# A Fourier-filter and gated-MLP block: small scale arithmetic moved to GpSimd, the first tiles transposed in fp32, and a later clock for DMA

## The chip, the cores and the metric

The kernel runs on one core of one Trainium2 chip. Five engines work side by side on it, each through a queue of its own in program order: TensorE (PE, matmuls into PSUM), VectorE (DVE), ScalarE (ACT), GpSimd (POOL) and SyncE (SP), which here issues all DMAs. The metric is device time in microseconds (us) of one execution. Three runs of the kernel before took 435.36, 435.87 and 436.03 us; the median, 435.87, is the time before.

## The reference

The input x has 2048 tokens of 448 values. Three terms are added:

```python
xn = (x - mean) / sqrt(var + 1e-5)                      # per token
y1 = irfft2(rfft2(xn) * (w_r + 1j * w_i))               # over tokens and features
gate, up = x @ W_gate, x @ W_up                         # of xn, 448 -> 1792
y2 = ((gate * (gate > 0)) * up) @ W_down                # 1792 -> 448
out = x + y1 + y2                                       # fp32
```

The gated MLP is fed with xn. All operands and the result are fp32.

## The kernel before

**Precision by halves.** A matrix is held as two fp16 parts, hi (the value rounded to fp16) and lo (the remainder). A product takes three fp16 matmuls, hi x hi, lo x hi and hi x lo. Weights are first scaled by a power of two, found from their sum of squares.

**The MLP.** The 1792 hidden features are 14 slabs f of 128, taken in groups of 5, 5 and 4. Tokens are 16 tiles n2 of 128, in four chunks q of four tiles (n2 = q, q+4, q+8, q+12), in the order 0, 2, 1, 3. A gate-and-up unit (`gu`) multiplies one slab with one chunk: for gate (g = 0) and up (g = 1) ten matmuls of 512 columns, and a group on half the rows (`gu_halves`) that two neighbouring units share. ScalarE and VectorE turn the sums into h (relu, product, hi, lo). When a group's slabs are done for a chunk, four down-projection units (`dn`) follow, one a tile. They add into a PSUM bank that ScalarE first seeds with the running output (`dn_seed`) and then reads back (`dn_post`).

**The filter.** The two-dimensional transform runs as small DFT matmuls (`f_dft`, `f_sdft`, `i_sdft`, `i_ddft`, PSUM tile fx) and butterflies on VectorE (tile y). It is background work, laid between the MLP's units.

**Tokens.** The MLP needs the normalized tokens transposed: `Tq[q]` holds nine blocks of 128 features by 512 tokens. Blocks 0 to 2 are hi, 5 to 7 lo; blocks 3, 4 and 8 hold the 64 last columns, their lo, and a strided choice of columns. For the first chunk (`CHUNKS[0]`, tiles 0, 4, 8, 12) TensorE transposes; for the other three a DMA does. The first chunk's steps before, named as in the list `OPENING`: `lx` load, `bn`, `ag` mean and variance, `sq` root on ScalarE, `ra` to `rm` the reciprocal root on VectorE in small steps (groups A: tiles 0, 4; B: 8, 12; C: chunk 2), `xn` (or `an` on ScalarE) the normalized tile, `hi` its fp16 half (on ScalarE, from the loaded tile), `lo` the remainder on VectorE, `tpA` and `tpB` three fp16 transposes each, `evA` and `evB` the copies out of PSUM, `tpC` and `evC0` to `evC2` the 64 last columns of all four tiles.

**The opening.** `OPENING` (line 34) is written out by hand: each engine runs the pieces of its own in that order. Weights of the first group: `lw` loads the next half slab, `wsqWfg` sums its squares on ScalarE, `parWf` adds them over partitions on GpSimd, `wexW` and `wscW` take the power of two on VectorE, `whiW` (ScalarE) and `wloW` (VectorE) write the halves. The first matmuls of slab 0 are cut into three 256-column ones each: `hh`, `lh`, `hl`, first digit g, second digit the half of the chunk; `ml` and `hp` handle the last columns. `guFgG` is ten matmuls of slab F. `re`, `tm`, `gh`, `gl` are the four steps to h. `lwd`, `wdq`, `wdp`, `wdsc`, `wdh`, `wdl` are the same for the down projection's weights. `warm` and `kw4` are matmuls on zeros.

**Behind the opening** a planner (`Order`, line 183) decides. It has a cost for each instruction, runs all queues against each other on paper (`place`), picks by due time and earliest start, and issues every instruction in the order that comes out. Cost and start time are its own estimates. A DMA counts as landed by `dma`; an instruction that needs it may start 0.04 us later (`lag`, line 317). How much background work is laid beside a unit follows from `V_US` and `room`.

Line 413 is the one line that issues all planned instructions, so the profile shows L413 nearly everywhere; groups are told apart by tile names. wst, wt: weight slabs as loaded and as halves; wdst, wdt: the same for the down projection; wds, dsc, dinv: its scales; wsc: a slab's power of two; xy: tokens and running output; T: `Tq`; arena: a shared area with, among others, the token tiles of the opening, constants and DFT tables; gu, dn, fx: PSUM.

Of the kernel before, what the change touches and what calls it, by code (L numbers as in the profile page):

```python
# [25 lines left out]
NWARM = 16  # L26
ARENA = 17072
HOLD = 3.0
# [6 lines left out]
lx0 lx4 bn0 lx12 bn4 lx8 lw ag0 lid lw ag4 sqA raA rbA rcA warm rdA rmA xn0 bn12 bn8 an4 ag12 hi0 ag8 lo0 hi4 sqB tpA0  # L35
wsqW0g0 lx14 lw tpB0 raB lo4 rbB rcB tpB4 kw4 rdB rmB aevA0 wsqW0g1 lw xn8 tpA4 parW0g0 wexW0g0 lx6 lw vevB4 hi8 vevB0
hi12 wscW0g0 vevA4 whiW0g0 lx10 tpA8 aevA8 tpA12 parW0g1 lo8 tpB8 wsqW1g1 hh00 hl00 wsqW1g0 lw lw lw xn12 vevA12 hh01
lo12 wexW0g1 wloW0g0 parW1 wscW0g1 tpB12 whiW0g1 vevB12 lx2 tpC aevC1 bn6 lwd3 lh01 lh00 wexW1 wscW1 vevB8 hh10 vevC0
whiW1g0 wloW0g1 hl10 wloW1g0 whiW1g1 wloW1g1 hl11 bn10 bn2 bn14 hh11 lwd0 wsqW3g1 ml0 ml1 wsqW2g0 wsqW2g1 lh11 wsqW3g0
parW2 lfd ag2 hl01 ag10 lh10 ag14 ag6 hp0 re0 tm0 lw lwd1 sqC raC wexW2 lw gu1g0 rbC wscW2 rcC rdC xn14 parW3 wexW3  # L40
whiW2g1 wloW2g1 lwd4 gu1g1 hi14 cp14 wscW3 xn2 whiW2g0 lo14 wloW2g0 whiW3g0 hi2 lwd2 whiW3g1 wsqW4g0 xn10 re1 wsqW4g1
parW4 wloW3g0 hi10 cp2 ly0 tm1 gu2g1 gu2g0 cp10 ly4 wdq0 wdq4 wloW3g1 wexW4 gh0 xn6 wdq3 lo10 hp2 gu3g0 hi6 re2 ly12
wscW4 whiW4g0 lo2 whiW4g1 gu3g1 lo6 wdq2 gh1 tm2 dm14 wdq1 gl0 wloW4g0 gu4g0 ly8 dm10 wloW4g1 gl1 cp6 gu4g1 re3 gh2
tm3 wdp wdsc gh3 gl3 aevC2 wdh1 dm2 gl2 wdl1 wdh4 dm6 wdh3 wdl4 hp4 re4 wdl3 tm4 wdh0 wdl0 wdh2 wdl2 gh4 gl4
# [60 lines left out]
def _constants():  # L105
# [55 lines left out]
    ident = np.eye(128, dtype=np.float16)  # L161
# [9 lines left out]
class _Node:  # L171
    __slots__ = ("eng", "ops", "key", "run", "fixed", "after", "wait", "users", "start", "ready", "late")
# [10 lines left out]
class Order:  # L183
# [5 lines left out]
    SWITCH = 0.093  # L189

    def __init__(self, hold):
        self.nodes, self.reads, self.writes, self.masks = [], {}, {}, {}
        self.key, self.after, self.fixed, self.group, self.hold, self.stream = 0.0, None, True, None, hold, []
# [17 lines left out]
    @contextmanager  # L211
    def run(self, back=True):
        n = self.node("P")
        n.run = back
        self.group = n
        yield n
        self.group = None
# [84 lines left out]
    def place(self):  # L302
# [37 lines left out]
        def pick(e):  # L340
# [25 lines left out]
            if h[1] > t + 0.5 or soon and (mode[0] != (128, 128) or now - n.ready > self.hold):  # L366
# [51 lines left out]
def tile_gfnet_reglu(ctx: ExitStack, tc: tile.TileContext, x, xr, wgu, wd, wf, ident, c_fd, c_fm, c_im, c_row, c_id,  # L418
                     out):
    nc = tc.nc  # L420
    order = Order(HOLD)
# [107 lines left out]
    id_t = ft([128, 128], F16, "id_t")  # L529
# [78 lines left out]
    def ln_r(step, q, js=(0, 1, 2, 3)):  # L608
# [3 lines left out]
        if step == "a":  # L612
            V.reciprocal(r0, sd)
        elif step == "b":
            V.scalar_tensor_tensor(t, m[:, :, 1], 1e-5, r0, op0=OP.add, op1=OP.mult)
        elif step == "c":
            V.scalar_tensor_tensor(t, t, -0.5 * 2048, r0, op0=OP.mult, op1=OP.mult)
        elif step == "d":
            V.scalar_tensor_tensor(r, t, 1.5 * 2048, r0, op0=OP.add, op1=OP.mult)
        elif q == CHUNKS[0]:  # L620
            V.scalar_tensor_tensor(nm, m[:, :, 0], -1.0, r, op0=OP.mult, op1=OP.mult)
        elif q in CHUNKS[2:]:
            V.tensor_scalar(nm, m[:, :, 0], -1.0, None, op0=OP.mult)
# [9 lines left out]
    for t in tts:  # L633
        G.memset(t[:, 3:9:5, 64:128], 0.0)
# [5 lines left out]
    def ln_xn(n2, act=False):  # L640
        xn_b[n2] = free.pop(0)
        xn[n2] = flat(xn_b[n2])[:, 0:D]
# [33 lines left out]
    def ln_lo(n2):  # L676
# [41 lines left out]
    def ln_ev(n2, part, act):  # L718
        q, j = n2 % 4, n2 // 4
        copy(Tq[q][:, 5 * part:5 * part + 3, 128 * j:128 * (j + 1)], tp[n2, part][:, 0:3], act)  # L720

    def ln_tpc(q):

        b = (fx(), fx())
        for i in range(3):
            tp["end", i] = b[i // 2].bitcast(F16)[:, 512 * (i % 2):512 * (i % 2) + 512]
        for j in range(4):
            t = tt[q + 4 * j].rearrange("p a b -> p (a b)")
            c, l = t[:, 384:448], t[:, 1024:1088]
            for i, half in enumerate(((c, t[:, 7:512:8]), (l, c), (l, t[:, 647:1152:8]))):  # L730
                for h in range(2):
                    P.transpose(tp["end", i][64 * h:64 * h + 64, 128 * j:128 * j + 128], half[h], id_t)

    def ln_evc(q, i, act):
        copy(Tq[q][:, (3, 4, 8)[i], :], tp["end", i], act)
# [412 lines left out]
    def i_ddft(a, b):  # L1148
# [6 lines left out]
        with order.run():  # L1155
# [78 lines left out]
    def wd_scale(g, fs):  # L1234
# [564 lines left out]
```

## Time and profile before

| | |
|---|---|
| median of three runs | 435.87 us (435.36 to 436.03) |
| the profiled execution | 435.47 us |
| its span, first to last instruction | 433.7 us |
| granted TensorE clock, mean | 0.999 |
| busy: PE, DVE, ACT, POOL | 425.0, 383.9, 262.6, 29.9 us |
| DMA | 38.63 MB, mean 89 GB/s |

A row of a timeline gives start, length, engine, line, operation, output<-input, shape and count of instructions that follow each other, and in brackets the engine's idle time ahead of it with what ended it. A row of groups gives a count, then the busy time in us and the mean of one in ns, then the idle time. A row of waits gives the total in us, the number of times and the longest. PEld is the loading of weights, which overlaps PE. Matmuls overlap as well: one of 512 columns lasts 0.379 us but the next starts 0.216 later.

### The profile page before, as it was taken

What the parts mean: (1) busy time and instruction counts of PE and PEld (TensorE: products, weight loads), DVE (VectorE), ACT (ScalarE), POOL (GpSimd) and SP (SyncE); (2) the same over time, 40 slices, a digit from 0 to 9 for tenths busy, and PEclk for the clock granted to TensorE, in tenths of its full rate; (3) what the DMA queues carried; (4) which work ended last, traced back from release to release, by engine and by line L of the source; (5) the groups of instructions that cost most, each with busy time, mean ns of one, the idle gap of its engine ahead of it and who ended that gap; (6) DMA issues with size and microseconds to landing.
All of it is one profiled execution on the core that took longest, in us unless ns stands there. A gap on an engine that the chain in (4) does not pass through costs nothing.

```text
span 433.7 us, 8470 instructions
## 1 busy us (share of the span) xinstructions
PE 425.0 (98%) x3222; PEld 202.7 (47%) x3222; DVE 383.9 (89%) x804; ACT 262.6 (61%) x495; POOL 29.9 (7%) x72
## 2 busy tenths in 40 slices
PE   7999999999999999999999999999999999999996
PEld 2644544444444444445444444444454554544554
DVE  6998989999998899899999999999999999973443
ACT  5898466387448658545534634764756765864761
POOL 1140013042000200000000000100000000000000
PEclk9999999999999999999999999999999999999999
DMA  8859319009104532342504200030222220210212
GB/s 259 297 123 264 127 46 239 7 14 227 42 3 132 182 101 86 89 127 79 158 14 108 82 1 0 16 86 2 51 47 50 73 74 16 80 44 2 85 44 87
DMA packets 37721, 38.63 MB, mean 89 GB/s; under 512 B 18928, under 2 KB 33072, under 8 KB 37680
## 3 DMA queue, kind: packets, MB, share of 16 engines
q1 hardware_dynamic: 37680, 38.09, 31.4%
q8 instruction: 25, 0.41, 0.4%
q14 instruction: 16, 0.13, 0.1%
HBM read 23.20 MB, written 3.67 MB: 62 GB/s over the span
## 4 chain that ended last, share of the span: by engine, by line
PE 42%; DVE 36%; issue 9%; ACT 4%; DMA 4%; SPq 2%; POOL 2%; DVEq 0%; ACTq 0%; POOLq 0%
PE gu L413 27%; DVE y L413 17%; PE dn L413 11%; DVE arena L413 5%; PE fx L413 4%; DVE g L413 3%; DVE h L413 3%; DVE wst L413 3%; SPq L413 2%; DVE wt L413 2%; POOL arena L413 2%; ACT arena L413 1%; DMA arena<-in_wf 1%; DMA xy<-in_x 1%; ACT junk L413 1%
## 5 line engine op out<-in xcount | busy, mean ns | idle before, releaser
L413 PE MATMUL gu<-T,wt 128*128 128x512 f16 (+2 forms) x1250 | 264.6, 376 | 0.0
L413 PEld LDWEIGHTS <-wt 128*128 128x128 f16 (+1 forms) x1250 | 111.3, 97 | 143.5 <-issue 20.9
L413 PE MATMUL dn<-wdt,h 128*128 128x448 f16 x648 | 125.6, 353 | 1.4 <-ACT dn L413 1.4
L413 PEld LDWEIGHTS <-h 128*128 128x128 f16 x684 | 66.0, 98 | 63.2 <-issue 4.1
L413 ACT ACTIVATE h<-g 128x512 f16<-128x512 f32 x56 | 35.1, 628 | 60.3 <-DVE g L413 59.9
L413 DVE TENSOR_TENSOR y<-y 128x464 f32<-128x464 f32 (+2 forms) x82 | 59.0, 745 | 2.7 <-ACT y L413 1.8
L413 DVE TENSOR_TENSOR arena<-arena 128x116 f32<-128x116 f32 (+6 forms) x105 | 53.2, 525 | 4.2 <-ACT arena L413 2.8
L413 DVE SCALAR_TENSOR_TENSOR g<-gu,g 128x512 f32<-128x512 f32 x56 | 38.3, 684 | 18.8 <-ACT g L413 15.8
L413 ACT ACTIVATE g<-gu 128x512 f32<-128x512 f32 x56 | 32.8, 586 | 32.4 <-PE gu L413 32.4
L413 DVE TENSOR_TENSOR h<-g,h 128x512 f16<-128x512 f32 x56 | 38.4, 687 | 4.4 <-ACT h L413 3.7
L413 ACT ACTIVATE xy<-dn,dsc 128x448 f32<-128x448 f32 x44 | 27.5, 626 | 19.4 <-PE dn L413 19.1
L413 DVE TENSOR_TENSOR wst<-wst 128x116 f32<-128x116 f32 (+2 forms) x96 | 30.8, 374 | 0.6
L413 DVE SCALAR_TENSOR_TENSOR y<-y 128x232 f32<-128x232 f32 (+2 forms) x52 | 30.1, 600 | 0.7
L413 ACT ACTIVATE dn<-xy,dinv 128x448 f32<-128x448 f32 x44 | 27.7, 636 | 1.9 <-DMA xy<-in_x 0.8
L413 PEld LDWEIGHTS <-arena 64*128 64x128 f16 (+2 forms) x836 | 17.1, 96 | 14.4 <-issue 5.5
L413 ACT ACTIVATE wt<-wst,wsc 128x512 f16<-128x512 f32 x28 | 18.9, 710 | 4.0 <-DVE wsc L413 4.0
L413 DVE SCALAR_TENSOR_TENSOR wt<-wst,wsc,wt 128x512 f16<-128x512 f32 x28 | 20.2, 744 | 0.1
L413 POOL COPY arena<-arena 128x56 f16<-128x56 f16 (+1 forms) x36 | 15.8, 474 | 59.7 <-ACT arena L413 53.8
L413 ACT ACTIVATE junk<-wst 128x512 bf16<-128x512 f32 x28 | 17.4, 622 | 3.5 <-DMA wst<-in_wgu 3.1
L413 ACT ACTIVATE arena<-arena 128x116 f32<-128x116 f32 (+3 forms) x33 | 14.9, 463 | 7.5 <-DMA arena<-in_wf 5.2
L413 POOL PARTITION_ALL_REDUCE wm<-wm x15 | 8.2, 547 | 158.4 <-ACT junk L413 158.4
L413 PE MATMUL fx<-arena 64*128 64x64 f16 (+3 forms) x484 | 17.8, 245 | 0.8 <-DVE T L413 0.5
(81 smaller groups left out, 294.6 us busy)
## 6 DMA issues: line engine op xcount, KB each, us to landing
wst<-in_wgu SPq DMA_DIRECT2D x28, 256.0 KB, 4.7
arena<-in_wf SPq DMA_DIRECT2D x16, 232.0 KB, 2.9
arena<-y SPq DMA_DIRECT2D x64, 58.0 KB, 2.0
arena<-wst SPq DMA_DIRECT2D x32, 116.0 KB, 2.2
y<-in_xr SPq DMA_DIRECT2D x16, 224.0 KB, 4.2
xy<-in_x SPq DMA_DIRECT2D x16, 224.0 KB, 3.6
out<-xy SPq DMA_DIRECT2D x15, 224.0 KB, 1.9
wdst<-in_wd SPq DMA_DIRECT2D x14, 224.0 KB, 3.4
```

Of the source, the lines that this page charges most:

```text
L413: fn(*a, **k)
```

## The change

Four things are done.

1. **First token tiles.** `xn` of tiles 0, 4, 8 and 12 stays fp32 in the memory of the fp16 tiles (`xts`). Three fp32 transposes a tile (`ln_tp`, identity now fp32, 64 KB) go to four PSUM banks; ScalarE's copy rounds to hi (`ath`), VectorE subtracts hi from PSUM for lo (`tl`). The 64 last columns take eight fp32 matmuls with the identity (`ln_tpc`), a copy (`aend0`), two subtractions (`end2`, `end3`) and one DMA inside SBUF (`end1`). `hi`, `lo`, `evA`, `evB`, `evC`, `an` of these tiles go. Zeroings are split: part stays at the start, one a tile (`z0` to `z3`) comes behind `tpC`.
2. **Small operations.** `shift_exponent` runs on GpSimd except for slabs 0 and 1. The root steps `rb` to `rm` of the chunks other than the first run there as one or two operations each. In `wd_scale` the products and maxima go there; the exponent, the reduction over features and the reciprocals stay on VectorE.
3. **The planner.** For an instruction behind the opening that is not a DMA itself, a DMA counts as landed 0.8 us after its estimate instead of 0.04 (`SLACK`). The hold time is given by kind of run, with the value of before for each; fp32 matmuls and 64-column ones get costs of their own; `V_US` gets smaller costs for the moved steps.
4. **The list.** `OPENING` is written anew: 10 warm-up matmuls instead of 16, `kw4` gone, other places for loads and weights.

```diff
-NWARM = 16
+NWARM = 10
-HOLD = 3.0
+HOLDS = 3.0, 3.0, 3.0, 3.0
...
 OPENING = """
+lx0 warm lx4 bn0 bn4 ag0 ag4 sqA raA rbA lx8 rcA rdA xn0 lx12 bn8 lw wsqW0g0 lid bn12 lw ag8 tp0 ag12 sqB xn4 wsqW0g1
+parW0g0 raB rbB ath0 lw wexW0g0 tp4 rcB rdB lw wscW0g0 xn8 whiW0g0 xn12 tp8 tl0 wloW0g0 parW0g1 tp12 rmA wsqW1g0 tpC
+ath4 wexW0g1 wsqW1g1 wscW0g1 whiW0g1 hh00 parW1 tl4 lh00 ath12 ath8 aend0 lx2 wexW1 hh10 wloW0g1 hl00 hh01 wscW1 tl8
+whiW1g0 hh11 tl12 lh11 whiW1g1 end2 wloW1g0 z2 wloW1g1 lwd3 lw lw lh01 lw lw wsqW3g1 hl11 lx6 lx14 end1 lx10 bn6 lwd0
+lwd2 wsqW2g0 lw lh10 wsqW2g1 hl10 parW2 bn10 bn2 hl01 wsqW3g0 z0 wexW2 ml1 bn14 ml0 hp0 ag2 parW3 wscW2 gu1g1 ag10 re0
+whiW2g1 lwd1 wexW3 ag14 ag6 sqC lw tm0 lfd wloW2g1 whiW2g0 raC wscW3 whiW3g0 rbC lwd4 rmB z3 rcC wsqW4g0 gu1g0 whiW3g1
+wloW2g0 wsqW4g1 rdC gu2g0 wloW3g0 xn14 hi14 z1 cp14 re1 wdq0 xn2 wloW3g1 lo14 ly4 parW4 xn10 tm1 hi2 cp2 hi10 wexW4
...
-    ident = np.eye(128, dtype=np.float16)
+    ident = np.eye(128, dtype=np.float32)
...
+    SLACK = 0.8
...
-            return max([d.end + 0.04 for d in op.deps if not (pe and d.node.eng == "P")], default=0.0)
+            far = 0.04 if op.node.eng == "S" or op.node.fixed else self.SLACK
+            return max([d.end + (far if d.node.eng == "S" else 0.04) for d in op.deps
+                        if not (pe and d.node.eng == "P")], default=0.0)
...
-    def shift_exponent(o, e, sign, n):
+    def shift_exponent(o, e, sign, n, E=G):
-        V.tensor_scalar(o.bitcast(U32), e.bitcast(U32), float(sign), n * EXPONE, op0=OP.mult, op1=OP.add)
+        E.tensor_scalar(o.bitcast(U32), e.bitcast(U32), float(sign), n * EXPONE, op0=OP.mult, op1=OP.add)
...
         elif step == "b":
-            V.scalar_tensor_tensor(t, m[:, :, 1], 1e-5, r0, op0=OP.add, op1=OP.mult)
+            G.tensor_scalar(t, m[:, :, 1], 1e-5, None, op0=OP.add)
+            G.tensor_tensor(t, t, r0, op=OP.mult)
         elif step == "c":
-            V.scalar_tensor_tensor(t, t, -0.5 * 2048, r0, op0=OP.mult, op1=OP.mult)
+            G.tensor_tensor(t, t, r0, op=OP.mult)
+            G.tensor_scalar(t, t, -0.5 * 2048, 1.5 * 2048, op0=OP.mult, op1=OP.add)
         elif step == "d":
-            V.scalar_tensor_tensor(r, t, 1.5 * 2048, r0, op0=OP.add, op1=OP.mult)
+            G.tensor_tensor(r, t, r0, op=OP.mult)
...
+    def ln_tp(n2):
+        j = n2 // 4
+        b = (side[1], *side[0], side[2])[j]
+        tp[n2] = b[:, 0:384].rearrange("p (a b) -> p a b", b=128)
         for a in range(3):
-            P.transpose(tp[n2, part][:, a, :], tt[n2][:, 5 * part + a, :], id_t)
+            P.transpose(tp[n2][:, a, :], xn[n2][:, 128 * a:128 * a + 128], id_t)
...
+    def ln_th(n2, act):
+        js = slice(128 * (n2 // 4), 128 * (n2 // 4) + 128)
+        copy(Tq[n2 % 4][:, 0:3, js], tp[n2], act)
+    def ln_tl(n2):
+        T, js = Tq[n2 % 4], slice(128 * (n2 // 4), 128 * (n2 // 4) + 128)
+        V.tensor_tensor(T[:, 5:8, js], tp[n2], T[:, 0:3, js], op=OP.subtract)
...
+        tp["end"] = side[1]
+        for j, x in enumerate(xts):
+            js = slice(128 * j, 128 * j + 128)
+            for h, c in ((0, slice(384, 448)), (1, slice(7, 512, 8))):
+                P.matmul(tp["end"][64 * h:64 * h + 64, js], x[:, c], id_t, start=j == 0, stop=True,
+                         skip_group_check=True)
+    def ln_end(q, i, act=False):
+        T, a = Tq[q], tp["end"]
+        if i == 0:
+            copy(T[:, 3, :], a, act)
+        elif i == 1:
+            Q.dma_start(T[64:128, 4, :], T[0:64, 3, :])
+        elif i == 2:
+            V.tensor_tensor(T[0:64, 4, :], a[0:64], T[0:64, 3, :], op=OP.subtract)
+        else:
+            V.tensor_tensor(T[:, 8, :], a, T[:, 3, :], op=OP.subtract)
...
-        V.tensor_tensor(sc[:, 0, 0:n], w[:, :, 0], w[:, :, 1], op=OP.mult)
-        V.scalar_tensor_tensor(sc[:, 1, 0:n], sc[:, 0, 0:n], 2.0 ** -64, e, op0=OP.max, op1=OP.mult)
+        G.tensor_tensor(sc[:, 0, 0:n], w[:, :, 0], w[:, :, 1], op=OP.mult)
+        G.tensor_scalar(sc[:, 1, 0:n], sc[:, 0, 0:n], 2.0 ** -64, None, op0=OP.max)
+        G.tensor_tensor(sc[:, 1, 0:n], sc[:, 1, 0:n], e, op=OP.mult)
         V.tensor_reduce(sc[:, 2, 0:1], sc[:, 1, 0:n], axis=AX.X, op=OP.max)
-        V.tensor_scalar(dsc[:, g:g + 1], sc[:, 2, 0:1], 2.0 ** -20, 2.0 ** -60, op0=OP.mult, op1=OP.max)
+        G.tensor_scalar(dsc[:, g:g + 1], sc[:, 2, 0:1], 2.0 ** -20, 2.0 ** -60, op0=OP.mult, op1=OP.max)
...
-    V_US = {"w_scale": 0.2, "w_lo": 0.66, "wd_scale": 1.1, "wd_lo": 0.6}
+    V_US = {"w_scale": 0.1, "w_lo": 0.66, "wd_scale": 0.7, "wd_lo": 0.6}
```

More of the change, by code (lines that the diff above doesn't have):

```diff
@@ L34 @@
 OPENING = """
[L35 to L44, printed above, removed]
+lx0 warm lx4 bn0 bn4 ag0 ag4 sqA raA rbA lx8 rcA rdA xn0 lx12 bn8 lw wsqW0g0 lid bn12 lw ag8 tp0 ag12 sqB xn4 wsqW0g1
[5 more added lines that the diff above has]
+wloW2g0 wsqW4g1 rdC gu2g0 wloW3g0 xn14 hi14 z1 cp14 re1 wdq0 xn2 wloW3g1 lo14 ly4 parW4 xn10 tm1 hi2 cp2 hi10 wexW4
+cp10 gh0 xn6 hi6 gu2g1 lo10 wscW4 ly12 lo2 hp2 re2 lo6 ly8 gh1 tm2 wdq4 gl0 dm14 dm10 wdq3 gl1 gu3g0 whiW4g0 wdq2 cp6
+whiW4g1 wloW4g0 gu3g1 end3 wdq1 wloW4g1 re3 gh2 tm3 wdp wdsc gh3 dm2 gu4g0 gu4g1 dm6 gl3 wdh1 gl2 ly0 wdl1 hp4 wdh4
+wdh3 wdl4 re4 tm4 wdl3 wdh0 wdl0 wdh2 gh4 gl4 wdl2
 """
@@ L171 @@
 class _Node:
-    __slots__ = ("eng", "ops", "key", "run", "fixed", "after", "wait", "users", "start", "ready", "late")
+    __slots__ = ("eng", "ops", "key", "run", "fixed", "after", "wait", "users", "start", "ready", "hold", "late")
 def _repeat(m, step, n):
@@ L189, with __init__ @@
     SWITCH = 0.093
-    def __init__(self, hold):
+    SLACK = 0.8
+    def __init__(self):
         self.nodes, self.reads, self.writes, self.masks = [], {}, {}, {}
-        self.key, self.after, self.fixed, self.group, self.hold, self.stream = 0.0, None, True, None, hold, []
+        self.key, self.after, self.fixed, self.group, self.stream = 0.0, None, True, None, []
     def engine(self, eng, real):
@@ L211, in run @@
     @contextmanager
-    def run(self, back=True):
+    def run(self, hold=None):
         n = self.node("P")
-        n.run = back
+        n.run, n.hold = hold is not None, hold
         self.group = n
@@ L365, in pick @@
             soon = t <= now + self.SWITCH + 0.01
-            if h[1] > t + 0.5 or soon and (mode[0] != (128, 128) or now - n.ready > self.hold):
+            if h[1] > t + 0.5 or soon and (mode[0] != (128, 128) or now - n.ready > n.hold):
                 return run
@@ L632, in tile_gfnet_reglu @@
     tts = [ft([128, 9, 128], F16, f"tt{i}") for i in range(4)]
-    for t in tts:
-        G.memset(t[:, 3:9:5, 64:128], 0.0)
+    xts = [t.rearrange("p a b -> p (a b)").bitcast(F32) for t in tts]
+    for t, u in zip(tts, xts):
+        G.memset(u[:, 448:512], 0.0)
+        G.memset(t[:, 8, 64:128], 0.0)
     def new_tt(n2):
@@ L640, in ln_xn @@
     def ln_xn(n2, act=False):
-        xn_b[n2] = free.pop(0)
-        xn[n2] = flat(xn_b[n2])[:, 0:D]
+        if n2 % 4 == CHUNKS[0]:
+            xn[n2] = xts[n2 // 4][:, 0:D]
+        else:
+            xn_b[n2] = free.pop(0)
+            xn[n2] = flat(xn_b[n2])[:, 0:D]
         r, nm, mean = rst[n2 % 4, n2 // 4, "r"]
@@ L716, in copy @@
             V.tensor_copy(o, i)
-    def ln_ev(n2, part, act):
-        q, j = n2 % 4, n2 // 4
-        copy(Tq[q][:, 5 * part:5 * part + 3, 128 * j:128 * (j + 1)], tp[n2, part][:, 0:3], act)
-    def ln_tpc(q):
[L724 to L735, printed above, removed]
+    def ln_th(n2, act):
[4 more added lines that the diff above has]
+        V.tensor_tensor(T[:, 5:8, js], tp[n2], T[:, 0:3, js], op=OP.subtract)
+    def ln_tpc(q):
+        tp["end"] = side[1]
[12 more added lines that the diff above has]
+            V.tensor_tensor(T[0:64, 4, :], a[0:64], T[0:64, 3, :], op=OP.subtract)
+        else:
+            V.tensor_tensor(T[:, 8, :], a, T[:, 3, :], op=OP.subtract)
     fi, sfx = {}, {}
@@ L776, in f_dft @@
         ps, T = fx2(), Tq[a % 4]
-        with order.run():
+        with order.run(HOLDS[0]):
             for k, n2 in enumerate((a, b)):
@@ L823, in f_sdft @@
         sfx[a] = ps
-        with order.run():
+        with order.run(HOLDS[1]):
             for k in range(2):
@@ L1030, in row_dft @@
         y = state["rowps"] = fx()[:, 0:NG * KC]
-        with order.run():
+        with order.run(HOLDS[0]):
             for a in range(2):
@@ L1113, in i_sdft @@
         sps[p] = ps
-        with order.run():
+        with order.run(HOLDS[2]):
             for b in range(2):
@@ L1154, in i_ddft @@
             A.activation(sides[e], xy2[:, a, :, 224 * e:224 * (e + 1)], AF.Copy, scale=fsc[:, 2:3])
-        with order.run():
+        with order.run(HOLDS[3]):
             for k, n2 in enumerate((a, b)):
@@ L1268, in gu_full @@
         for g in gs:
-            with order.run(False):
+            with order.run():
                 for i, (a, b) in enumerate(seq):
@@ L1288, in gu_halves @@
         gu_open(*mate)
-        with order.run(False):
+        with order.run():
             for i in range(4):
@@ L1333, in dn_mm @@
         js = slice(128 * j, 128 * (j + 1))
-        with order.run(False):
+        with order.run():
             for f in fs:
@@ L1367, in dn_end @@
             js = slice(128 * (n2 // 4), 128 * (n2 // 4 + 1))
-            with order.run(False):
+            with order.run():
                 for i, (a, b) in enumerate(((0, 0), (0, 1), (1, 0))):
@@ L1678, in tile_gfnet_reglu @@
     G.memset(warm, 0.0)
-    wps = dn_bank(), dn_bank()
+    side[1], side[2] = dn_bank(), fx()
+    wps = dn_bank(), fx()
     side[0] = gu_bank()
```

64 lines of the change are left out of this document (29 added, 35 removed).

## The prediction

> **What bounds the kernel now.** I read the page first: shares of busy time, then the chain that ended last.
>
> ```profile
> span 433.7 us, 8470 instructions
> PE 425.0 (98%) x3222; PEld 202.7 (47%) x3222; DVE 383.9 (89%) x804; ACT 262.6 (61%) x495; POOL 29.9 (7%) x72
> PE 42%; DVE 36%; issue 9%; ACT 4%; DMA 4%; SPq 2%; POOL 2%; DVEq 0%; ACTq 0%; POOLq 0%
> ```
>
> The two disagree: TensorE is busy 98% of the span, yet a third of the chain runs over VectorE. The view of who waits for whom decides, because it shows what TensorE itself lost.
>
> ```profile
> PE dn L413 <- POOL arena L413: 1.9, 1, 1.9
> PE dn L413 <- ACT dn L413: 1.4, 2, 0.9
> PE gu L413 <- DVE arena L413: 1.1, 3, 0.5
> PE fx L413 <- DVE T L413: 0.5, 1, 0.5
> PE fx L413 <- ACT y L413: 0.3, 1, 0.3
> PE fx L413 <- ACT arena L413: 0.2, 1, 0.2
> ```
>
> In 433.7 us TensorE waited 5.4 us, and 3.7 us of it is the first wait and the three with arena and T as releasers, all in the opening. Behind the opening only 1.7 us are left. So TensorE's queue of work sets the end, and an edit is worth what it does to the moment at which useful matmuls begin to run without a break, plus any wait it puts into the queue later. The timeline of TensorE shows that moment (start, length, group, count):
>
> ```profile
> 1.89 5.63 PE L413 MATMUL dn<-arena 128*128 128x512 f16 x16 [1.89 <-POOL arena L413]
> ...
> 9.37 1.03 PE L413 MATMUL dn<-arena 128*128 128x512 f16 x4
> ...
> 12.30 1.15 PE L413 MATMUL gu<-T,wt 128*128 128x256 f16 x9
> ...
> 13.69 1.37 PE L413 MATMUL fx<-arena 128*64 128x128 f16 x24
> 14.99 22.81 PE L413 MATMUL gu<-T,wt 128*128 128x256 f16 x121
> 37.64 0.82 PE L413 MATMUL fx<-arena,T 64*128 64x58 f16 x48
> 38.39 4.49 PE L413 MATMUL gu<-T,wt 128*128 128x512 f16 x20
> ```
>
> The groups at 1.89 and 9.37 are warm-up on no data, those with fx<-arena are transposes. Useful work is the 9 matmuls at 12.30 and everything from 14.99. From there to the first forward transform (37.64) no wait is marked. A 512-column matmul takes (4.49 - 0.16) / 20 = 0.216 us, 0.16 being the tail of the last; a 256-column one (1.15 - 0.16) / 9 = 0.109.
>
> **The change part by part.** *Transposes.* Before, a token tile of the first chunk passes four steps on ScalarE and VectorE (the normalized values, their fp16 half, the remainder, two copies out of PSUM), and its 64 last columns a further transpose group. After, one normalization, a transpose in fp32, a copy out on ScalarE that rounds (ath) and a subtraction on VectorE (tl). These rows have the prices:
>
> ```profile
> 8.13 0.28 ACT L413 ACTIVATE arena<-arena,eps 128x2 f32<-128x2 f32 x1
> 8.32 0.61 ACT L413 ACTIVATE junk<-wst 128x512 bf16<-128x512 f32 x1
> 8.84 0.18 ACT L413 ACTIVATION_READ_ACCUMULATOR junk<-wst 128x1 f32 x1
> 8.93 0.47 ACT L413 ACTIVATE T<-fx 128x384 f16<-128x384 f16 x1
> ...
> 15.59 1.32 ACT L413 ACTIVATE wt<-wst,wsc 128x512 f16<-128x512 f32 x2
> ```
>
> ```profile
> L413 ACT ACTIVATE arena<-y,arena 128x448 f16<-128x448 f32 x4 | 2.8, 746 | 0.0
> ...
> L413 DVE SCALAR_TENSOR_TENSOR wt<-wst,wsc,wt 128x512 f16<-128x512 f32 x4 | 2.8, 743 | 0.0
> L413 DVE TENSOR_TENSOR arena<-y,arena 128x448 f16<-128x448 f32 x4 | 2.4, 607 | 0.0
> L413 DVE TENSOR_SCALAR y<-y,arena 128x448 f32<-128x448 f32 x4 | 2.0, 509 | 0.0
> 5.38 0.75 DVE L413 SCALAR_TENSOR_TENSOR arena<-arena 128x2 f32<-128x2 f32 x4
> ```
>
> The fp32 transpose stands nowhere in the trace. Its nearest rows are the fp32 matmuls of the second transform, eight instructions of 464 columns in four quarters of the array, hence two passes, and the fp16 transposes, whose smallest price is 128 / 2 of a 256-column matmul, 0.055 us:
>
> ```profile
> 123.68 1.01 PE L413 MATMUL fx<-arena 64*64 64x464 f32 x8
> L413 PEld LDWEIGHTS fx<-arena 64*64 64x64 f32 x64 | 1.7, 131 | 3.3 <-issue 1.6 <-ACT g L413 0.4 <-ACT junk L413 0.4
> ```
>
> (1.01 - 0.16) x 128 / 464 = 0.23 us for 128 columns in both passes. From above, 0.49, if both passes wait for a weight load of 0.131 (a gain is not excluded below: 0.055). I take 0.23, the row of the same type, whose second loads lay under its first pass: 0.70 a tile, and 4 x 0.23 = 0.93 for the 64 last columns, whose two halves run side by side.
>
> Now the chain that opens the useful work. The queue of SyncE has eight transfers in flight; from the ninth on, an issue tells when the one eight before landed. The last two rows price a transfer between partitions and the half-row matmuls:
>
> ```profile
> 7.37 0.33 SPq L413 DMA_DIRECT2D y<-in_xr  x1
> 7.74 1.58 SPq L413 DMA_DIRECT2D wst<-in_wgu  x3
> arena<-y SPq DMA_DIRECT2D x64, 58.0 KB, 2.0
> L413 PE MATMUL gu<-T,wt 64*128 64x512 f16 x112 | 17.0, 381 | 0.0
> ```
>
> So the first weight slab landed at 7.37 and the identity by 7.74; both keep their places in the queue (the identity doubles to 64 KB; I put 0.1 on it, hidden, for tile 0 is normalized at 6.5). ScalarE takes the squares of that slab first (0.52 + 0.09 to the next start), then the second root, to 8.27; four small steps of VectorE at (0.75 - 0.16) / 3 = 0.2 from start to start, 9.07; the normalization of tile 8, 9.6; its transposes, 10.3, those of tile 12, 11.0; the last columns, 12.0 (they reuse tile 0's bank, which VectorE has read by 10.7). Useful matmuls then run in one piece: 36 x 0.109 + 2 x 0.216 + 17.0 / 28 = 0.6 (the half-row group hp0) make 5.0, to 17.0. Do the inputs keep up? ScalarE has, from 7.37: four squares 2.5, a root 0.2, four copies 1.5 (0.47 less the 0.09 by which neighbours overlap), two weight halves 1.3, the copy of the last columns 0.5, two weight halves 1.3: slab 1 is ready at 14.7, and VectorE's remainders of 0.74 follow by 16.1, ahead of hp0 (16.4). It drops one normalization of 0.76 and four of 0.746; before, the same slab was ready at 15.59 + 1.32 = 16.9. One new transfer (end1) carries half of the last columns to other partitions: it waits in SyncE's queue for ScalarE's copy at 13.4 and lands 2.0 later, at 15.4, 0.5 ahead of its reader. Queued behind it stand a token tile (lx10), two weights of the down projection and slab 4; their readers come at 17 to 21 us, so the cover is thin only for lx10.
>
> Before, the 18.5 us of matmuls between hp0 and 37.64 (80 x 0.216 and two half-row groups) put its end at 19.2. The formula, from 14.99 with the 27 matmuls left, says 19.0, and the old opening worked out by its list as above begins them at 14.7. I add the 0.5 that this lacks: 17.5 after, 1.7 earlier.
>
> *Small operations on GpSimd.* The root steps of chunk 2 become five operations in a row there, the weight powers of slabs 2 to 13 one each, the down projection's scales eight, with VectorE between. No such operation is in the trace. Nearest are its small copies:
>
> ```profile
> 24.20 0.81 POOL L413 COPY arena<-arena 128x56 f16<-128x56 f16 x1 [0.61 <-DVE arena L413]
> ...
> 30.12 0.29 POOL L413 COPY arena<-arena 128x56 f16<-128x56 f16 x1 [0.55 <-DVE arena L413]
> 24.12 0.74 DVE L413 SCALAR_TENSOR_TENSOR wt<-wst,wsc,wt 128x512 f16<-128x512 f32 x1
> ```
>
> 0.29 us alone; but the one that started at 24.20, under a VectorE instruction with two SBUF inputs that ran to 24.86, ended at 25.01. I take 0.25 alone (below 0.16 a step, VectorE's own, a gain) and up to 0.81 under such an instruction. The Trainium skill, SBUF — State Buffer, Who interferes with whom, says that a VectorE instruction with two SBUF inputs and a GpSimd instruction that reads SBUF exclude each other; the trace agrees (0.81 against 0.29), and by that rule the moved steps aren't free however small they are.
>
> In the opening the five root steps of chunk 2 take 5 x 0.28 = 1.4 alone. VectorE's two remainders of 0.74, next in its list behind the reciprocal, hold up the first two: 2.3. VectorE then stands at the normalization that waits for them, with slab 3's last remainder queued behind it. Slab 4's halves then come late; TensorE would wait 0.8 to 1.0 for them by my list, where the same list for before has 0.7 that the trace does not show. I charge 0.4. The scales before the first down projection become eight steps of 0.25 and four of 0.2 with VectorE idle between, 2.8 against 2.2 for eleven steps of 0.2 before; VectorE's list ahead of them has become shorter by the moved steps (thirteen at 0.08 to 0.2) and by 0.607 less 0.53 a tile, so I charge nothing. Four zeroings that move behind the transposes stand in GpSimd's queue among the root steps; they are in the 2.3.
>
> *Later clocks, constants.* The later landing of DMAs changes only the order in which the program's planner writes instructions down; it can move the 1.7 us of late waits either way: 0. Fewer warm-up matmuls cost nothing as TensorE has nothing else until 7.6. HOLDS repeats the old value; smaller V_US lets background work start a little earlier, order again.
>
> Sum: 435.47 (the profiled execution: span 433.7 and 1.77 around it) - 1.7 + 0.4 = 434.2; the median of three is 0.4 above it, so 434.6.
>
> **The rivals.** *A: the clock of TensorE falls back (no gain).* Warm-up shows its rate:
>
> ```profile
> 1.89 1.46 PE L413 MATMUL dn<-arena 128*128 128x512 f16 x3 [1.89 <-POOL arena L413]
> 5.71 1.81 PE L413 MATMUL dn<-arena 128*128 128x512 f16 x7
> ```
>
> Three in 1.46 is 0.43 apiece, half rate, while the page grants full clock; near the second row it changes to 0.216. Ten at 0.43 end at 6.2, and until 12.0 there are only transposes, where before four more warm-up matmuls stood at 9.37. If it falls back, 3.8 us (1.89 to 5.7) at half rate lose 1.9 us: 436.5. For it: 3.7 us of transposes in 5.8; against: before, gaps of 0.4 to 0.5 did no harm. The Trainium skill, TensorE: Matmul & The Clock Gate, Parts 1 and 4, gives a free-running window of about 3.4 us and says that transposes don't count as busy; by it this is the case.
>
> *B: GpSimd's steps stand in the way later (slower).* Here the second group's scales were ready just in time:
>
> ```profile
> 168.28 1.23 ACT L413 ACTIVATE wdt<-wdst,wds 128x448 f16<-128x448 f32 x2
> ...
> 170.52 0.64 ACT L413 ACTIVATE dn<-xy,dinv 128x448 f32<-128x448 f32 x1
> 171.21 1.48 PE L413 MATMUL dn<-wdt,h 128*128 128x448 f16 x7 [0.50 <-ACT dn L413]
> ```
>
> ScalarE runs wdt as soon as the scales exist, then the seed that TensorE already waits for. If seven GpSimd steps of that chain each wait 0.55 behind VectorE, the seed is 3.9 late, every bit on TensorE; with every other one 1.9, and 436.9 with 0.4 for the third group. It outweighs the gain from 1.3 us on. Against: the planner may put other work between.
>
> *C: the start is not handed on.* The chain's 36% on VectorE would be the true bound, and TensorE, early, waits for it in the transforms: 435.9. Against: 1.7 us of waits in 420.
>
> *D: the late waits go too*, if seeds wait for token loads that the planner counted as landed too early: up to 1.4 more, 433.2. *E: the fp32 transposes cost 0.49.* Tiles then end at 9.2, 10.7, 12.2, 13.6, the last columns at 15.6, hp0 at 21.1: 1.9 late, 437.8.
>
> **How the numbers follow.** Forecast 0.43, A 0.14, B 0.12, C 0.14, D 0.12, E 0.05. The forecast's own range is 433.8 (transposes at the fp16 price, nothing lost to slab 4) to 435.4 (1.0 lost there, 0.2 on the transposes). A measurement tells 0.2% (0.9 us) from no change: under 435.0 is faster, over 436.7 slower. Faster: four fifths of the forecast, D, and a little of the others where D's gain comes on top, 0.48; same: the rest of the forecast, C, A, 0.36; slower: B and E, 0.16. Range: 433.2 (D) to 436.9 (A and the middle of B).
>
> **What would show it.** Transposes of three in about 0.9 with tail; hp0's successors from 17.6; the first transform near 36.3; slab 4 the only new wait of the opening. GpSimd rows of 0.2 to 0.3 alone and up to 0.8 in the later stages. Wrong if useful matmuls begin after 13 or run at 0.22 per 256 columns (A), if TensorE's waits on ACT dn or on wdt grow beyond 1.4 (B), or if waits on fx appear (C).

## The result, and the profile after

The changed kernel takes 505.92 us (median of 6 runs, 504.8 to 508.38) beside 435.75 for the kernel before: ratio 1.1622 (95% interval 1.1602 to 1.1642). I had forecast 434.6. The profiled execution took 504.8 us, with a span of 502.9.

The page of the changed kernel, the same rows as shown of before, and the clock:

```profile
span 502.9 us, 8449 instructions
...
PE 441.6 (88%) x3192; PEld 205.8 (41%) x3192; DVE 378.2 (75%) x755; ACT 258.7 (51%) x491; POOL 48.8 (10%) x134
...
PEclk9977857999999998999999999977979999999999
...
PE 39%; DVE 23%; issue 15%; ACT 7%; DMA 6%; SPq 5%; POOL 3%; POOLq 0%; DVEq 0%; ACTq 0%
```

TensorE is no longer full, no other engine is, and "issue" (time in which the engine waited for nothing that the profile shows) has grown from 9% to 15% of the chain. The view of waits says who waits for whom (engine and tile, releaser; us in total, times, longest):

```profile
ACT wt L416 <- POOL wsc L416: 36.1, 5, 9.1
POOL wsc L416 <- issue: 32.9, 4, 9.5
ACT wdt L416 <- POOL wds L416: 27.0, 3, 18.4
...
POOL ed L416 <- issue: 18.4, 2, 11.5
...
PE dn L416 <- ACT dn L416: 17.0, 2, 14.6
PE gu L416 <- ACT wt L416: 15.7, 2, 9.0
```

Read it from the last two rows upwards: TensorE waits for ScalarE, ScalarE for the scales that GpSimd makes, and GpSimd for nothing that the profile shows. In before, no wait of TensorE behind the opening was over 0.9. All waits of TensorE together rose from 5.4 to 58 us, and its idle time from 8.7 to 61.3. Its busy time rose by 16.6 (425.0 to 441.6) with fewer matmuls. 52.6 more idle and 16.6 more busy are the 69.2 us by which the span grew.

The timeline of GpSimd shows what these gaps are (start, length, group; idle time before it in brackets):

```profile
17.92 0.40 POOL L416 PARTITION_ALL_REDUCE wm<-wm  x1 [0.26 <-ACT junk L416]
27.75 0.45 POOL L416 TENSOR_SCALAR wsc<-eg 128x2 uint32<-128x2 uint32 x2 [9.44 <-issue]
...
40.49 0.41 POOL L416 PARTITION_ALL_REDUCE wm<-wm  x1 [5.88 <-issue]
40.78 1.74 POOL L416 COPY arena<-arena 128x56 f16<-128x56 f16 x5
49.52 0.18 POOL L416 TENSOR_SCALAR wsc<-eg 128x2 uint32<-128x2 uint32 x1 [7.00 <-issue]
49.77 0.90 POOL L416 COPY arena<-arena 128x56 f16<-128x56 f16 x4
56.76 0.46 POOL L416 PARTITION_ALL_REDUCE wdm<-wdm  x1 [6.10 <-issue]
68.71 0.20 POOL L416 TENSOR_SCALAR ed<-ed 128x5 uint32<-128x5 uint32 x1 [11.48 <-issue]
```

Each time that GpSimd goes from the cross-partition sum (PARTITION_ALL_REDUCE) to ordinary arithmetic, or back, it stands still for 5.9 us at least; between a sum and a copy, or arithmetic and a copy, there is no gap. The compiled program has a sign of it too: on GpSimd's list stands an instruction without operands at each such place, 22 of them here (one ahead of the first sum, 21 at a change) and before only the one ahead of the first sum, where nothing waited for it:

```
L416 ISA wm_101<-wm_101 128x2
L416 ISA
L416 TENSOR_SCALAR wsc_105<-eg 128x2
```

In the compiled program it bears the name `PseudoReloadLibraryIndex`, with index 1 ahead of a sum and 0 ahead of arithmetic. The name speaks of a load of code. The transfers don't show one: the page's two rows of instruction transfers have 25 and 17 packets here, 25 and 16 before.

What this does to TensorE stands in its timeline:

```profile
50.52 0.61 PE L416 MATMUL gu<-T,wt 128*128 128x512 f16 x1 [9.00 <-ACT wt L416]
...
77.45 8.11 PE L416 MATMUL dn<-wdt,h 128*128 128x448 f16 x30 [14.56 <-ACT dn L416]
...
86.25 5.85 PE L416 MATMUL dn<-wdt,h 128*128 128x448 f16 x30
```

The wait at 50.52 ends the chain sum 40.49, power 49.52, weight half. The wait at 77.45 ends the chain sum 56.76, scales from 68.71. And the same 30 matmuls take 8.11 us after that wait and 5.85 the next time. The windows give the reason (start:end, length, busy time and instructions of TensorE first, granted clock as PEclk):

```profile
77.00:79.00 2.00, 1.55 (x5) 0.65 (x5) 1.61 (x4) 2.00 (x4) 0.00 (x0) 0.50 0.00 0
79.00:81.00 2.00, 2.00 (x7) 0.78 (x6) 1.97 (x4) 0.34 (x1) 0.00 (x0) 0.50 0.00 0
81.00:83.00 2.00, 2.00 (x9) 0.89 (x8) 1.93 (x5) 0.18 (x1) 0.00 (x0) 0.73 0.00 0
83.00:85.00 2.00, 2.00 (x12) 1.01 (x11) 1.86 (x7) 1.09 (x2) 0.00 (x0) 1.00 0.00 0
```

After this wait TensorE runs at half its clock for over 4 us, so a stall is paid for twice. The clock row of the page falls to 5 to 8 tenths in the slices of the long waits. In all the stretches with a clock of 0.5 TensorE was busy for 35.9 us; half of that, 18 us, is my estimate of what the lower clock cost, enough for the 16.6.

The opening, which by the forecast gains 1.7 us, in TensorE's timeline:

```profile
7.80 0.52 PE L416 MATMUL dn<-arena 128*128 128x128 f32 x3 [1.40 <-DVE arena L416]
...
10.32 0.86 PE L416 MATMUL fx<-arena 128*128 128x128 f32 x3
11.11 1.99 PE L416 MATMUL dn<-arena 128*64 128x128 f32 x16
13.03 9.87 PE L416 MATMUL gu<-T,wt 128*128 128x256 f16 x62
```

Three transposes took 0.52 us with the tail of the last at first, and 0.86 later: the clock fell back on the way. Useful matmuls start at 13.03; the first forward transform, at 37.64 before, comes at 57.65, behind the waits for scales.

My theory: GpSimd loads other code whenever it changes between the sum and arithmetic (a switch, below), at 6 to 7 us or more, and nothing else of the change costs much. The rivals: the small steps themselves are slow on GpSimd (in conflict with VectorE, or in their hand-overs); or the fp32 transposes and the new opening take a good part.

### The profile page after: what moved, and what is told of

The parts are those of the page before. It is cut to its first block, busy times and chain, and to the rows that moved or that the text cites. A ratio compares the mean times of both kernels' runs of the same rounds, so it can differ in the third digit from the quotient of the medians.

```text
span 502.9 us, 8449 instructions
## 1 busy us (share of the span) xinstructions
PE 441.6 (88%) x3192; PEld 205.8 (41%) x3192; DVE 378.2 (75%) x755; ACT 258.7 (51%) x491; POOL 48.8 (10%) x134
## 4 chain that ended last, share of the span: by engine, by line
PE 39%; DVE 23%; issue 15%; ACT 7%; DMA 6%; SPq 5%; POOL 3%; POOLq 0%; DVEq 0%; ACTq 0%
PE gu L416 21%; PE dn L416 14%; DVE y L416 12%; SPq L416 5%; PE fx L416 4%; DVE arena L416 3%; DVE g L416 2%; DVE wt L416 2%; DVE h L416 2%; DMA wst<-in_wgu 1%; DMA arena<-y 1%; ACT wt L416 1%; DVE wst L416 1%; POOL arena L416 1%; ACT h L416 1%
## 5 line engine op out<-in xcount | busy, mean ns | idle before, releaser
L416 PE MATMUL gu<-T,wt 128*128 128x512 f16 (+2 forms) x1250 | 278.7, 389 | 27.9 <-ACT wt L416 15.7
L416 PEld LDWEIGHTS <-wt 128*128 128x128 f16 (+1 forms) x1250 | 114.4, 100 | 183.9 <-issue 52.2
L416 PE MATMUL dn<-wdt,h 128*128 128x448 f16 x648 | 128.4, 357 | 17.0 <-ACT dn L416 17.0
L416 ACT ACTIVATE wdt<-wdst,wds 128x448 f16<-128x448 f32 x14 | 8.7, 656 | 27.0 <-POOL wds L416 27.0
L416 PE MATMUL fx<-arena 64*128 64x64 f16 (+2 forms) x456 | 19.7, 256 | 2.6 <-DVE arena L416 2.6
L416 PEld LDWEIGHTS <-arena 64*128 64x128 f16 (+1 forms) x778 | 13.6, 96 | 12.8 <-issue 4.6
```

The lines of the kernel that those rows point to most:

```text
L416: fn(*a, **k)
```

## The experiments

**back_on_vector**: the changed kernel with the moved steps in their old form.

```
-    def shift_exponent(o, e, sign, n, E=G):
+    def shift_exponent(o, e, sign, n, E=V):
...
-            G.tensor_scalar(t, m[:, :, 1], 1e-5, None, op0=OP.add)
-            G.tensor_tensor(t, t, r0, op=OP.mult)
+            V.scalar_tensor_tensor(t, m[:, :, 1], 1e-5, r0, op0=OP.add, op1=OP.mult)
```

> The changed kernel with every moved sum and product back on VectorE, in the form that it had before (root steps, weight powers, the scales of the down projection); fp32 transposes, written-out opening, later DMA clock and constants stay as changed. Theory (code load: GpSimd pauses 6 to 7 us each time it goes from the cross-partition sum to ordinary arithmetic or back, 21 times): the whole loss of 70 us goes; waits of TensorE fall from 58 us to about 5, and the time is 435 (434.3 to 436.3), because the opening's own gain, read from the changed trace as 0.6 us, stays. Rival 1 (the fp32 transposes or the new opening cost a good part of the loss, for instance by a lower TensorE clock): 440 or more. Rival 2 (the gain forecast for the opening is there in full once slab 4 is in time): 433.8.

Measured: 435.51 us (434.02 to 437.58, 12 runs), ratio 1.0 (0.9988 to 1.0012). The whole loss is gone, so all of it came with the moved steps, and rival 1 falls. Rival 2 falls too, and the 0.6 us that the theory left to the opening do not show. TensorE's waits are back to 4.6 us in the profiled execution, the fastest of the twelve.

**sums_left_out**: one kind of code.

```
-        G.partition_all_reduce(o, i, 128, bass_isa.ReduceOp.add)
+        G.tensor_scalar(o, i, 1.0, None, op0=OP.mult)
```

> The changed kernel with all arithmetic left on GpSimd as the change put it, and the 19 cross-partition sums left out: in place of each stands a GpSimd multiplication by one, so every partition scales by its own sum of squares. That leaves GpSimd one kind of code. Theory (code load): no pause of 6 us is left, the waits of TensorE on scales fall under 10 us in all, and the time is 437 (434 to 441), a little above the version with the steps on VectorE because GpSimd's steps run up to 0.8 us under VectorE. Rival (GpSimd's steps themselves, or their hand-overs with VectorE, or their conflict for SBUF make the loss): all of these are still there, so the time stays above 490.

Measured: 437.41 us (437.29 to 437.51), ratio 1.0041 (1.0028 to 1.0054). The same scales that started at 68.71 in the changed kernel, in its timeline:

```profile
32.77 0.39 POOL L416 TENSOR_SCALAR wdm<-wdm 128x5 f32<-128x5 f32 x1 [2.89 <-ACT junk L416]
34.05 0.20 POOL L416 TENSOR_SCALAR ed<-ed 128x5 uint32<-128x5 uint32 x1 [0.90 <-DVE ed L416]
...
36.56 1.20 POOL L416 TENSOR_SCALAR wds<-wds 128x5 f32<-128x5 f32 x1 [0.30 <-DVE wds L416]
```

1.3 us from the stand-in for the sum to the first step, not 12. With every moved step still on GpSimd, 68.5 of the 70 us are gone: the steps are not slow, the change of kind is. What the steps cost here, with the stand-ins for the sums, is 437.41 - 435.51 = 1.9 us; one that runs beside VectorE takes up to 1.20 in place of 0.2.

**probe_product** and **probe_copy**: the price without any dependence.

```
         G.partition_all_reduce(o, i, 128, bass_isa.ReduceOp.add)
+        k = state["sums"] = state.get("sums", -1) + 1
+        kind = '------sssssssssssss'[k] if k < 19 else ""
+        if kind == "s":
+            G.tensor_scalar(probe, eps, 1.0, None, op0=OP.mult)
...
+        elif kind == "c":
+            G.tensor_copy(probe, eps)
...
```

`k` counts the sums; probe_copy has `c` in place of each `s`. In both, a buffer (`small`) has 48 columns instead of 64.

> The kernel before, with one product of a single column (input constant, result read by nobody) put on GpSimd behind each of 13 of its 19 cross-partition sums. Theory (code load): the pauses appear with no dependence at all: about 22 of them of 6 to 7 us each, so about 140 us of GpSimd stand still with nothing to wait for; since the code for the next sum is loaded as soon as the product is done, sums are late only where the next one follows within some 13 us, and GpSimd's copies and sums behind a load are late; so far less than 70 us is lost: 445 (437 to 470). Rival (the pauses in the changed kernel are waits for VectorE or for a semaphore that the profile doesn't show): product and sum follow one another within 1 us, and the time is 435.9, as before.

> The same 13 probes as copies of one column instead of products. Theory (code load, and copies belong to no loaded code): no pause, the time stays within 0.2% of before: 435.9 (435.2 to 436.6). Rival (any extra instruction between two sums costs a pause): about the same time as with products.

Measured: with products 469.55 us (467.78 to 470.43), ratio 1.0774 (1.0751 to 1.0797); with copies 435.95 (435.04 to 436.49), ratio 1.0004 (0.9994 to 1.0014). GpSimd's timeline, products first:

```profile
122.17 0.46 POOL L413 PARTITION_ALL_REDUCE wm<-wm  x1 [5.79 <-issue]
129.42 0.41 POOL L413 TENSOR_SCALAR probe<-eps 128x1 f32<-128x1 f32 x1 [6.80 <-issue]
135.85 0.41 POOL L413 PARTITION_ALL_REDUCE wm<-wm  x1 [6.02 <-ACT y L413]
143.46 0.38 POOL L413 TENSOR_SCALAR probe<-eps 128x1 f32<-128x1 f32 x1 [7.21 <-issue]
```

```profile
133.88 0.41 POOL L413 PARTITION_ALL_REDUCE wm<-wm  x1 [18.98 <-ACT junk L413]
134.16 0.25 POOL L413 COPY probe<-eps 128x1 f32<-128x1 f32 x1
```

A product that reads a constant, and whose result nobody reads, starts 7 us late; a copy in its place starts at once. So the gap is no wait for data. The gap of 6.02 in the third row has the same length, though the profile names ScalarE as its releaser: the pause itself is in no list of the profile. The 34 us lie at the upper edge of what I expected. TensorE's waits say where:

```profile
PE dn L413 <- ACT dn L413: 16.5, 1, 16.5
PE fx L413 <- DVE arena L413: 13.2, 1, 13.2
```

Two long waits, not many short ones: GpSimd's queue runs in order, so a pause holds up sums that stand behind it and that others read.

**powers_only**, **scales_only**, **roots_only**: back_on_vector with one group of steps on GpSimd, each with the lines of the changed kernel.

> The version with all steps back on VectorE, but the weight powers of slabs 2 to 13 (12 single instructions) on GpSimd as the change has them. The compiled program then switches GpSimd's code 16 times between sum and arithmetic, against 21 in the changed kernel. Theory (each switch costs 6 to 7 us of GpSimd, whatever runs behind it): by its share of the switches 16/21 of the 70 us, 53, hence 489; since a power's slab has some slack, 465 to 490. Rival (the loss goes with the number of operations moved, 12 of some 53): 16 us, 451.

> The version with all steps back on VectorE, but the scales of the three groups of the down projection (8 instructions each) on GpSimd as the change has them. 7 switches of code in the compiled program. Theory (switches): 7/21 of 70 us, 23, hence 459 (445 to 465), with the longest waits of TensorE on ACT dn and of ScalarE on the scales wds. Rival (number of operations, 24 of some 53): 32 us, 467; rival of the record (each GpSimd step waits 0.55 us behind VectorE, no pauses): 437 to 440.

> The version with all steps back on VectorE (and the 10 cold warm-up matmuls), but the root steps of chunks 2, 1 and 3 (17 instructions) on GpSimd as the change has them. 4 switches of code in the compiled program. Theory (switches, 2.4 to 3.3 us each as in the powers and the scales alone): 445 to 449. Rival (number of operations, 17 of some 53): 22 us, 457.

| version | switches | operations | us | ratio (interval) | lost per switch |
|---|---|---|---|---|---|
| powers_only | 16 | 12 | 473.72 | 1.0867 (1.0842 to 1.0892) | 37.9 / 16 = 2.4 |
| scales_only | 7 | 24 | 456.46 | 1.0468 (1.0443 to 1.0493) | 20.6 / 7 = 2.9 |
| roots_only | 4 | 17 | 449.26 | 1.0309 (1.0288 to 1.0331) | 13.6 / 4 = 3.4 |
| the change | 21 | 54 | 505.92 | 1.1622 (1.1602 to 1.1642) | 70.2 / 21 = 3.3 |

Twelve single instructions cost nearly twice as much as 24 in three blocks. The loss goes with the number of switches, not of operations: the rival missed all three times. The theory's ranges held for powers_only and scales_only; roots_only came out 0.3 above its own (445 to 449). By the theory, how much of a switch reaches TensorE depends on the time that its reader has to spare. In scales_only the eight steps of the first two groups have one pause in front of them; the third group's are split by a sum and have two. This pause stands in the middle of a chain that TensorE waits for. The timeline of GpSimd there, for the first group:

```profile
34.17 0.54 POOL L416 PARTITION_ALL_REDUCE wdm<-wdm  x1 [3.31 <-ACT junk L416]
43.73 0.20 POOL L416 TENSOR_SCALAR ed<-ed 128x5 uint32<-128x5 uint32 x1 [9.03 <-issue]
```

**warm_more**: what became of the opening.

```
-NWARM = 10
+NWARM = 16
...
-... xn8 whiW0g0 xn12 tp8 ...
+... xn8 whiW0g0 xn12 kw4 tp8 ...
```

> The version with all steps back on VectorE, with 16 warm-up matmuls at the start in place of 10 and four more between the fp32 transposes of tiles 4 and 8, to keep TensorE busy until useful work begins. Theory (the clock of TensorE fell back during the transposes, and the gain in the opening was lost to that): transposes stand 0.11 us apart in place of 0.21, the last columns take 1.0 us in place of 2.0, useful matmuls begin at 12.2 in place of 13.4 and run at 0.109 from the first; the first forward transform is at 36.2 in place of 37.3, and the time 434.4 (1.1 less). Rival (the inputs from ScalarE and VectorE bind, not the clock): matmuls start earlier but wait for weight halves, and the time stays at 435.5.

Measured: 433.95 us (433.2 to 434.41), ratio 0.9952 (0.994 to 0.9965). TensorE's timeline of back_on_vector, then of warm_more:

```profile
5.79 0.63 PE L416 MATMUL fx<-arena 128*128 128x512 f16 x1
7.96 0.88 PE L416 MATMUL dn<-arena 128*128 128x128 f32 x3 [1.55 <-DVE arena L416]
8.63 0.85 PE L416 MATMUL gu<-arena 128*128 128x128 f32 x3
...
11.43 1.99 PE L416 MATMUL dn<-arena 128*64 128x128 f32 x16
13.36 24.07 PE L416 MATMUL gu<-T,wt 128*128 128x256 f16 x130
37.26 0.82 PE L416 MATMUL fx<-arena,T 64*128 64x58 f16 x48
```

```profile
7.07 0.38 PE L416 MATMUL dn<-arena 128*128 128x512 f16 x1
...
7.93 0.49 PE L416 MATMUL dn<-arena 128*128 128x128 f32 x3
8.26 0.49 PE L416 MATMUL gu<-arena 128*128 128x128 f32 x3
...
10.56 1.25 PE L416 MATMUL dn<-arena 128*64 128x128 f32 x16
11.74 9.71 PE L416 MATMUL gu<-T,wt 128*128 128x256 f16 x63
21.93 14.37 PE L416 MATMUL gu<-T,wt 128*128 128x512 f16 x67 [0.48 <-DVE wt L416]
36.14 0.81 PE L416 MATMUL fx<-arena,T 64*128 64x58 f16 x48
```

Three transposes take 8.63 - 7.96 = 0.67 us from start to start in the one and 0.33 in the other, the last columns 1.99 and 1.25. Useful work starts 1.6 earlier, and 1.1 of that is left at the first transform (0.5 goes to the wait for slab 2). Back_on_vector's warm-up ended before the clock had risen: its last matmul still lasts 0.63 us, where warm_more's last ones last 0.38. So the transposes went by at half rate. This differs between executions: in that of the changed kernel, after the same ten, the first transposes still ran at full rate (0.52). With ten more matmuls on no data the time is 1.9 us under before, where back_on_vector's is that of before; from 435.51 to 433.95 it is 1.6.

**constants_alone** and **slack_alone**: the planner's edits on the kernel before; the second has only the later DMA clock (`SLACK = 0.8`), the first the smaller `V_US` as well.

> The kernel before with the planner's edits alone: DMAs counted as landed 0.8 us later, and the smaller times for the scales; the opening, the transposes and GpSimd as before. Theory (order only, no work): within 0.2%: 435.6 (434.8 to 436.5). Rival (the late waits of 1.7 us go, which the profile of the version with the steps on VectorE suggests, as it gains 1.1 us behind the opening): 434.5.

> The kernel before with the later DMA clock alone. Theory (the gain of 1.6 us of the planner's two edits comes from the later clock, which puts instructions that wait for a load behind others): 434.3. Rival (it comes from the smaller times for the scales, which let background work start earlier): 435.8.

Measured: 434.29 us (433.64 to 434.56), ratio 0.996 (0.9947 to 0.9972), and 434.58 (two of its eleven executions were far off, at 448.29 and 1133.92), ratio 0.9974 (0.9965 to 0.9984). The rival of the first holds and the theory of the second: the later clock alone gives most of it. What the smaller `V_US` adds is not shown, for the two intervals overlap. TensorE's waits on the seeds fell from 1.4 us to this, of constants_alone:

```profile
PE dn L416 <- ACT dn L416: 0.7, 1, 0.7
```

That is 0.7 of the 0.9 us by which the profiled spans differ (433.7 and 432.8); the runs say 1.6. I can't place the rest.

**opening_alone**: warm_more with the planner's constants of before (`SLACK = 0.04`, the old `V_US`).

> The opening of the changed kernel kept warm (16 + 4 warm-up matmuls), all steps on VectorE, and the planner's constants as before (DMAs counted as landed with the data, the old times for the scales). Theory (the two gains lie in different places: 1.5 us in the opening, some 0.9 to 1.5 behind it): first forward transform at 36.1, time 434.4, 1.5 less than before. Rival (the transforms and seeds behind the opening don't take the earlier start, so that only the constants gained): 435.6.

Measured: 435.69 us (434.24 to 436.96), ratio 1.0 (0.999 to 1.0009). The rival holds. The first transform starts at 36.89, 0.75 before the old one, and then TensorE waits:

```profile
PE dn L416 <- ACT dn L416: 2.2, 2, 1.3
...
PE fx L416 <- ACT y L416: 1.2, 1, 1.2
PE gu L416 <- DVE g L416: 0.8, 1, 0.8
```

Against before 0.8 more on the seeds (ACT dn), 0.9 on a transform, 0.8 on VectorE: the earlier start is waited away later. With the later DMA clock these waits are gone (in warm_more 1.1 on the seeds, nothing on the other two). The sizes are those of single executions, the slowest of twelve here (436.96) and the fastest of five in warm_more (433.2); the medians alone say that the opening gains nothing by itself.

**best**: an attempt to beat warm_more by its wait for slab 2.

```
-... parW2 bn10 bn2 hl01 wsqW3g0 z0 wexW2 ml1 bn14 ml0 hp0 ag2 parW3 wscW2 gu1g1 ...
+... parW2 bn10 wexW2 wscW2 bn2 hl01 wsqW3g0 z0 ml1 bn14 ml0 hp0 ag2 parW3 gu1g1 ...
```

> The kept-warm version, with the scale of slab 2 taken by VectorE one token tile earlier in the written-out opening (two small instructions ahead of two statistics of tokens). In the kept-warm version TensorE waited 0.5 us at 21.9 for the low half of slab 2, and ScalarE stood from 18.1 to 19.2 until that scale was there. Theory: that wait goes, first transform at 35.7, time 433.5, 0.4 less than kept warm. Rival (the token tiles that are now later come late instead): 434.0 or more.

Measured: 434.32 us (433.26 to 435.26), ratio 0.9971 (0.9961 to 0.998). No better, as the rival has it: in its profile TensorE still waits 0.4 us for that slab and 2.0 for the seeds. The lowest median is warm_more's: transposes, opening and later DMA clock of the change, the old warm-up, and the small steps left on VectorE. But its interval (0.994 to 0.9965) overlaps with that of constants_alone (0.9947 to 0.9972), so no run shows that the fp32 transposes and the new opening add anything to the planner's edits.

## Why the prediction was wrong

**The step that failed** is the price of the small operations on GpSimd: "No such operation is in the trace. Nearest are its small copies", 0.25 us alone and up to 0.81 under VectorE, and 0.4 us charged in all. The moved steps cost 505.92 - 435.51 = 70.4. For the operation itself the price was near: 0.18 to 0.27 alone, up to 1.2 under VectorE, 1.9 us in the sum where only one kind of code is in the queue. But I asked what stands beside GpSimd's steps (VectorE) and what waits in its queue, not what kind of instruction stands ahead of them there. The sums were in the trace of before, each a few instructions from where a moved step would go. A copy was the wrong nearest row: copies go with the sum without a gap. That the trace showed no ordinary arithmetic on GpSimd at all, in a kernel that uses it for other things, should have opened the bound upwards. Rival B named the right place (seeds and weight halves behind GpSimd's steps, waits on ACT dn beyond 1.4) with the wrong price: 0.55 us a step behind VectorE, where a switch costs 6 to 12. The Trainium skill, GPSIMD Engine Reference, 2.1 Instruction dispatch, says that the first call to freshly loaded code costs an extra load of about 6 us that no instruction of the profile shows. The trace agrees with the size (5.8 to 8.2 us mostly, up to 11.9) and with its not being shown; an estimate by that sentence would have been 21 x 6 = 126 us of GpSimd. What the runs show is that the pause belongs to the change of kind; that it is a load of code is the reading of that sentence and of the bare instruction's name in the program.

**Transposes.** I took 0.23 us for 128 fp32 columns, two passes. Measured: 0.11 at full clock, 0.22 at half. The last columns were forecast at 0.93; they take 1.25 with the tail of the last, and 1.99 at half clock. The rows count three instructions for three transposes but sixteen for the eight matmuls of the last columns, so the two passes hold for the fp32 matmul and not for the transpose.

**The opening.** Useful matmuls were forecast from 12.0, and 0.5 of bias on top. They came at 13.0 in the changed kernel and 13.4 in back_on_vector, because rival A held, to which I had given 0.14: half clock. With the clock held up they start at 11.74, and the first transform at 36.14 is where I had put it (36.3). "Fewer warm-up matmuls cost nothing" was wrong by 1.6 us (435.51 against 433.95). What rival A cites from the Trainium skill, TensorE: Matmul & The Clock Gate, Parts 1 and 4, agrees with the traces as far as they go: the transposes of back_on_vector ran at half rate throughout and did not raise the clock, and in the changed kernel it fell during them. No run tells the transposes from the gaps between them (1.40 and 1.14 us in the changed kernel).

**Handed on?** Rival C held for the opening by itself (opening_alone: ratio 1.0), and rival D for the constants (1.6 us, of which I had given 1.4 as a rival and 0 in the sum). Without the moved steps the change takes 435.51, 0.9 above the forecast and inside its range; with the old warm-up too, 433.95. But the sum was near only by errors that cancel: the opening was priced at a gain of 1.7 and gives nothing alone, the constants at nothing and give 1.6.

## What to carry to other kernels

Before work moves to GpSimd, list what its queue would hold in order: each change between a cross-partition sum and an ordinary product was a pause of about 6 us or more here, which the trace of a kernel without such pairs can't show; keep such an engine to one kind, or use copies and fills only. An operation that is missing from an engine's trace has no nearest row there, and its price is bounded by a probe (here one product behind each sum), not by the cheapest relative. Warm-up work ahead of a critical stretch is part of that stretch: if it shrinks, read the spacing of the next matmuls, not their count.

## What the runs showed of the hardware

- A change between PARTITION_ALL_REDUCE and arithmetic (TENSOR_SCALAR, TENSOR_TENSOR) on GpSimd costs 5.8 to 8.2 us as a rule: 6.7 to 8.2 from the sum to arithmetic, mostly 5.8 to 6.9 back. COPY and MEMSET go with either. Some gaps behind a sum were 8.9 to 11.9 (at 27.75 and 68.71 in the changed kernel, 11.89 in powers_only); why was not tried.
- After a wait of 14.56 us TensorE ran at a granted clock of 0.50 for over 4 us: 8.11 us for work that takes 5.85.
- At the start of the span the clock row of the page shows full speed while matmuls stand at half rate (0.67 us for three transposes in back_on_vector); the spacing tells, the row doesn't.
- An fp32 transpose of 128 columns takes 0.11 us at full clock (three in 0.33 in warm_more), half of what the fp32 matmul rows of before suggested.
